# Weight conversion with its low bits taken by ScalarE, head 0 multiplied in plain float32, and a new set of due times

## The chip, the core and the metric

The kernel runs on one core of one Trainium2 chip. The metric is the device time of one execution in microseconds (us). The engines are named as the profile names them: PE is TensorE's matmul, PEld its weight load, DVE is VectorE, ACT is ScalarE, POOL is GpSimd, SP is SyncE, which issues the transfers (DMA).

## What is computed

Two batches of eight heads, 768 tokens of 64 numbers, go through an attention that is masked by clusters, and its output goes through two feed-forward stages. All weights (w1, w2, w3, w_out, w_in and w_out of the second stage) arrive as float64 and are turned into float32 on the chip.

```python
q_assign = argmax(einsum('bhsd,hcd->bhsc', q_n, c_n))      # 16 centroids per head
k_assign = argmax(einsum('bhsd,hcd->bhsc', k_n, c_n))
mask = q_assign[:, :, :, None] == k_assign[:, :, None, :]
scores = where(mask, scale * q @ k^T, -1e9)
attn = softmax(scores)
x = (attn @ v)                 # 1536 tokens x 512
h = (x @ w1) * (x @ w2) @ w3   # d_ff 1024
x = h @ w_out
h = x @ w_in                   # second stage, d_ff 2048
out = (h * clip(h + 3, 0, 6) / 6) @ w_out
```

## The kernel before

Nearly every float32 operand of a matmul is split into a high part (fp32r, written by ACT, sometimes POOL) and a low part (operand minus high part, written by DVE or POOL). A product of two split operands is three matmuls (high-high, high-low, low-high), a product with one split operand is two.

**The attention, per head** (`prep_ops`, `attn_ops`; 16 heads). q and k are transposed on PE (L1171), split (L1178, L1181), the cluster codes are worked out on DVE and POOL (L1224 to L1240). For each of six blocks of 128 queries, `scores` (L1309) fills 768 columns of PSUM, `smax` takes the maximum on DVE (L1321), `sexp` the exponentials on ACT (L1328). The probabilities are transposed on PE in nine groups of four 128x128 blocks (`p_T`, L1344). `p_hi` (L1346) copies each group to the fp32r tile `ph` on ACT, `p_lo` (L1351) writes the rest to `pl` on DVE; both move 128x512. `v_hi` and `v_lo` (L1158, L1164) put the high part of v in one half of the 128 columns of the tile `vs` and the low part in the other. `av` (L1354) multiplies: six calls for each head, in each two blocks, each with `ph` and with `pl`, so 24 matmuls of 384 columns for a head.

**The weights** (`conv_ops`, L1525). 72 tiles of 128x512 float64 numbers: 8 of w_out ("wo"), 16 of w3, 16 of w1 and w2 ("ab"), 32 of the second stage ("set"). A tile is loaded into `raw` (two 32-bit words a number), and then goes through five instructions: `c_bias` (c0, ACT) scales the high word, read as a float, into `cvt`; `c_clamp` (c1, POOL or DVE) clamps it in place; `c_shift` (c3, DVE, L1544) shifts it left by 3 into `cvs`; `c_low` (c4, DVE, L1548) ors in the low word shifted right by 29; `c_sign` (c5, DVE, L1552) ors in the sign. `raw`, `cvt` and `cvs` have two buffers each. c4 gives the `raw` buffer back (six tiles of w_out lie in a larger `rawx`), c5 gives back `cvt`. In the program, c3, c4 and c5 carry `lock=True`: the planner doesn't let them start while it thinks POOL is at work.

**The stages.** The weights w3 and w_out of the first feed-forward stage are multiplied with each other (`w_mm`, L1599) and the products of x with w1 and w2 (`ab_mm`, L1675) are made for batch 0 while the attention still runs (to about 384 us). Then come the two x2 products (`x2_mm`, L1790), batch 1's first stage (`b_mm`, L1927), and from 511 us on the second stage (`h_mm`, L2238, and `o_mm`, L2282). `idle_pe` (L1096) are matmuls without use, placed at the start.

**The order.** Each step is declared with `op` (key, engine, planned duration, what it needs, a due time, the buffers that it takes and gives back). `Plan.order` (L868) lays all steps out one by one: of the steps that can start at about the earliest time on each engine it takes the one with the earliest due time. A due time is a formula plus an entry of the table `SHIFT` (L44), some 3,700 numbers. The resulting order is fixed in the program: each engine runs its instructions strictly in that order. Steps declared with `fop` may go to more than one engine, as `RUN_ON` allows, and the planner chooses; c1 has "dp" (DVE or POOL).

Of the kernel before, what the change touches and what calls it, by code (L numbers as in the profile page):

```python
# [8 lines left out]
F32 = mybir.dt.float32  # L9
F32R = mybir.dt.float32r  # L10
I32 = mybir.dt.int32
AF = mybir.ActivationFunctionType
# [32 lines left out]
    "id": -11.08, "root": 17.17, "z": -42.97, "cenl": -6.79, "cen1": 13.45, "cen2": -5.32, "cen3": -2.8,  # L45
    ("idle", 0): 18.01, ("idle", 1): -7.42, ("idle", 2): -8.49, ("idle", 3): -0.46, ("idle", 7): 0.9,
    ("idle", 8): -9.34, ("cT", 0): -4.5, ("cTc", 0): -13.8, ("cTc", 1): -0.45, ("lq", 0): -10.38, ("lk", 0): -53.5,
    ("lv", 0): -30.2, ("vhi", 0): -8.63, ("vlo", 0): 28.32, ("T", 0, 0): -49.19, ("qkh", 0, 0): -18.28,
    ("qkl", 0, 0): -25.79, ("T", 0, 1): -28.46, ("qkh", 0, 1): -31.56, ("qkl", 0, 1): 15.3, ("Dk", 0): -25.47,
# [2340 lines left out]
```

## Time and profile before

| | |
|---|---|
| device time, median of 3 runs | 769.05 us (767.98 to 769.82) |
| the profiled execution | 768.52 us, of which the span from the first to the last instruction is 766.7 us |
| busy in the span | PE 737.8, PEld 673.3, DVE 648.0, ACT 511.1, POOL 212.0 us |
| mean granted TensorE clock | 0.994 of full speed |
| HBM read, written | 71.34 MB, 15.78 MB |

A group of instructions is shown with its line in the program, its engine, what it writes and reads, how many there are, the sum of their time and the mean of one; then the idle time of the engine just before them and who ended it. Many copies share the lines L990 (DVE subtraction) and L993 (ACT copy), since helpers issue them; they are told apart by their tiles. The ends of matmuls are modelled, and two that overlap in PE's pipeline each show their full length, so the time that a matmul takes of PE is read from how many follow each other in a stretch.

### The profile page before, as it was taken

Reading aid. Unit: us, or ns where it says so; the run is one execution under the profiler, and the core shown is the slowest. Engines: PE = TensorE matmul, PEld = TensorE weight load, DVE = VectorE, ACT = ScalarE, POOL = GpSimd, SP = SyncE. Lnnn points to the kernel's source line nnn. Section 1 sums busy time; section 2 is a strip of 40 time slices with the busy share of each in tenths; the row PEclk is TensorE's granted clock in tenths of the full one; section 3 lists DMA queues with packets and bytes.
Section 4 is the critical chain, followed back from the end, with each engine's and each line's share of the span. In section 5 each row is a group of like instructions: output and inputs, shape, how many; then the busy total and the mean of one; then the engine's idle time right before and its main releaser. Section 6 shows DMA issues by size and latency. Waiting matters only on the chain.

```text
span 766.7 us, 12083 instructions
## 1 busy us (share of the span) xinstructions
PE 737.8 (96%) x4143; PEld 673.3 (88%) x4143; DVE 648.0 (85%) x1114; ACT 511.1 (67%) x963; POOL 212.0 (28%) x233
## 2 busy tenths in 40 slices
...
PEclk9899999999999999999999999999999999999999
...
GB/s 241 187 139 128 130 156 150 107 128 143 115 203 130 194 161 146 139 110 68 136 121 152 179 97 165 105 225 140 164 163 153 111 121 168 97 42 42 71 12 83
DMA packets 81741, 101.97 MB, mean 133 GB/s; under 512 B 30960, under 2 KB 56592, under 8 KB 81680
## 3 DMA queue, kind: packets, MB, share of 16 engines
...
q14 instruction: 28, 0.23, 0.1%
HBM read 71.34 MB, written 15.78 MB: 114 GB/s over the span
## 4 chain that ended last, share of the span: by engine, by line
PE 80%; DVE 11%; ACT 3%; issue 2%; DMA 2%; POOL 0%; SPq 0%; DVEq 0%; ACTq 0%
PE po L2282 15%; PE psh L2238 13%; PE psx L1790 8%; PE psab L1675 8%; PE psab L1927 7%; PE pst L1309 7%; PE av L1361 7%; PE ptr L1344 6%; PE psw L1599 4%; DVE pl L990 2%; DVE den L1321 2%; DMA abp<-cvs 1%; PE pa L1210 1%; PE ptqk L1171 1%; DVE cvs L1548 1%
## 5 line engine op out<-in xcount | busy, mean ns | idle before, releaser
L1539 POOL TENSOR_SCALAR cvt<-cvt 128x512 f32<-128x512 f32 x72 | 70.4, 980 | 238.1 <-ACT cvt L993 207.9
L1328 ACT ACTIVATE p<-pst,den 128x768 f32<-128x768 f32 x96 | 86.6, 902 | 29.6 <-DVE den L1321 29.0
L1321 DVE TENSOR_REDUCE den<-pst 128x1 f32<-128x768 f32 x96 | 91.1, 949 | 13.4 <-PE pst L1309 10.1
L990 DVE TENSOR_TENSOR pl<-ptr,ph 128x512 fp32r<-128x512 f32 x144 | 96.2, 680 | 6.8 <-ACT ph L993 6.3
L993 ACT ACTIVATE ph<-ptr 128x512 fp32r<-128x512 f32 x144 | 83.4, 596 | 26.5 <-PE ptr L1344 23.5
L1344 PE MATMUL ptr<-id_f,p 128*128 128x128 f32 x576 | 82.1, 272 | 2.7 <-DVE pl L990 2.7
L1675 PE MATMUL psab<-xT,abhl 128*128 128x384 f32 x384 | 80.1, 343 | 2.5 <-DVE g L1685 2.5
L1344 PEld LDWEIGHTS ptr<-id_f,p 128*128 128x128 f32 x576 | 68.5, 140 | 9.6 <-issue 3.5
L1309 PE MATMUL pst<-kk,qkL 128*128 128x512 f32 (+1 forms) x192 | 71.0, 376 | 3.7 <-ACT p L1328 2.8
L1675 PEld LDWEIGHTS psab<-xT,abhl 128*128 128x128 f32 x384 | 65.7, 188 | 5.2 <-DVE g L1685 3.7
L1361 PE MATMUL av<-ph,vs 128*128 128x384 f32 x192 | 67.8, 353 | 0.5 <-issue 0.4
L1361 PE MATMUL av<-pl,vs 128*128 128x384 f32 x192 | 65.2, 340 | 2.1 <-DVE pl L990 2.1
L1309 PE MATMUL pst<-kk,qkH 128*128 128x512 f32 (+1 forms) x192 | 64.8, 341 | 1.9 <-ACT kk L993 1.9
L993 ACT ACTIVATE cvt<-raw 128x512 f32<-128x512 f32 x72 | 48.3, 673 | 13.1 <-DMA raw<-in_moe_w_dram 6.5
L1548 DVE SCALAR_TENSOR_TENSOR cvs<-raw,cvs 128x512 int32<-128x512 int32 x72 | 51.1, 713 | 0.5
L1552 DVE SCALAR_TENSOR_TENSOR cvs<-cvt,cvs 128x512 int32<-128x512 int32 x72 | 50.6, 705 | 0.3
L1599 PE MATMUL psw<-woh,wT 128*128 128x512 f32 x128 | 50.0, 409 | 0.2 <-DVE wT L990 0.2
L993 ACT ACTIVATE m_sn<-psh 128x384 f32<-128x384 f32 x64 | 31.0, 484 | 28.5 <-PE psh L2238 28.3
L2260 ACT ACTIVATE tt<-m_sn,three 128x384 f32<-128x384 f32 x48 | 29.4, 616 | 28.7 <-DVE m_sn L2248 19.7
L1544 DVE TENSOR_SCALAR cvs<-cvt 128x512 int32<-128x512 int32 x72 | 37.7, 527 | 11.1 <-POOL cvt L1539 4.2
L1309 PEld LDWEIGHTS pst<-kk,qkL 128*128 128x128 f32 x192 | 36.4, 189 | 10.9 <-ACT p L1328 8.9
L2282 PE MATMUL po<-m_hl,m_gv 128*128 128x512 f32 x171 | 43.8, 391 | 0.0
...
## 6 DMA issues: line engine op xcount, KB each, us to landing
...
```

Of the source, the lines that this page charges most:

```text
L990: nc.vector.tensor_tensor(out=out, in0=a, in1=b, op=ALU.subtract)
L993: nc.scalar.activation(out=out, in_=in_, func=AF.Copy, **kw)
L1309: x = mm(out=psr[:, t, ks_], lhsT=TT[nm, h][:, i, cs_], rhs=flat(TT["K", h][:, a])[:, ks_], start=st, stop=sp)
L1321: done["mx", n] = [other_banks(nc.vector.tensor_reduce(out=den_at(h, 0, c), in_=psS[h, c], axis=AX.X, op=ALU.max, negate=True), ("S", n + 1))]
L1328: done["ex", n] = [other_banks(nc.scalar.activation(out=flat(p), in_=psS.pop((h, c)), func=AF.Exp, bias=den_at(h, 0, c), accum_out=den_at( ...
L1344: nc.tensor.transpose(pt[:, blk(j)], pps[h, 3 * hf + c][:, blk(kb)], id_f)
L1361: mm(out=t[:, 0:HF], lhsT=vs_t[h][:, 2 * s + i, :], rhs=x_[:, c0:c0 + HF], start=(s == 0 and i == 0 and n == 0), stop=(s == 2 and i == 1 a ...
L1539: (nc.gpsimd.tensor_scalar if e == "pool" else ts)(out=tf, in0=tf, scalar1=H_MAX, scalar2=-H_MAX, op0=ALU.min, op1=ALU.max)
L1599: mm(out=ps, lhsT=wT[m, hf][:, a, blk(kk)], rhs=w_[hf][:, kk, :], start=(kk == 0 and n == 0), stop=(kk == 3 and n == 2))
L1675: mm(out=ps[:, 0:HF], lhsT=s[:, w, a, blk(kk)], rhs=xT0[0][:, x_, kk, hf * HF:hf * HF + HF], start=(kk == 0 and n == 0), stop=(kk == KD - ...
L2238: mm(out=ps[:, 0:HF], lhsT=left(p, l, a, kk), rhs=x[:, x_, kk, :], start=(st and kk == 0 and m == 0), stop=(kk == 1 and m == 2), skip_grou ...
L2282: mm(out=outs[b, c], lhsT=g[:, a, blk(c % 3)], rhs=w[:, w_, :], start=(first and a == 0 and w_ == 0), stop=(last and a == 1))
```

## The change

1. `c_low` moves from DVE to ACT and becomes step c2: it reads the top byte of the low word as an 8-bit integer (`raw` as bytes, every eighth byte), computes byte/32 - 15.5/32 and writes the result, rounded to an integer, into `cvs`. It needs c0, takes the `cvs` buffer and gives back `raw`. `c_shift` (c3) now both shifts the high word and ors the result with what c2 wrote, one instruction with two inputs, and so needs c1 and c2. c5 follows c3. DVE has two instructions for a tile where it had three, ACT two where it had one.
2. Head 0 (`WHOLE = 1`): `p_all` copies each transposed group to a float32 tile `p32` on ACT (in place of `p_hi`), there is no `p_lo`, v is copied whole to a float32 `vs` and the other half of the columns is set to zero by a POOL memset (in place of `v_lo`), and `av` is one float32 matmul for each block in place of two fp32r ones: 12 for 24. The group's PSUM buffer is given back by the ACT copy.
3. The second q/k transpose of a head is ordered after the first (`after=[("T", h, 0)] * hf`).
4. Every number of the table `SHIFT` is another one, so the fixed order of all engines is laid out anew.

```diff
     def v_hi(e, h):
-        t = at.tile([128, NC, 128], F32R, tag="vs", name="vs", bufs=2)
+        t = at.tile([128, NC, 128], F32 if h < WHOLE else F32R, tag="vs", name="vs", bufs=2)
...
     def v_lo(e, h):
         hi, lo = 64 * (h % 2), 64 - 64 * (h % 2)
+        if h < WHOLE:
+            nc.gpsimd.memset(vs_t[h][:, :, lo:lo + 64], 0.0)
+            return
         sub_on(e, vs_t[h][:, :, lo:lo + 64], v_n[h], vs_t[h][:, :, hi:hi + 64])
...
+    def p_all(h, n):
+        if not P32:
+            P32.append(at.tile([128, 1536], F32, tag="p32", name="p32"))
+        copy_act(P32[0][:, p_cols(n)], phl.pop((h, n)))
...
-            for n, x_ in enumerate(PHL):
+            ps_ = P32 if h < WHOLE else PHL
+            for n, x_ in enumerate(ps_):
                 mm(out=t[:, 0:HF], lhsT=vs_t[h][:, 2 * s + i, :], rhs=x_[:, c0:c0 + HF],
...
+        def c_low(e):
+            s = cvo[key] = base.tile([128, 512], I32, tag="cvs", name="cvs", bufs=2)
+            copy_act(s, raws.pop(key).bitcast(U8)[:, :, 3], scale=1.0 / 32.0, bias=-15.5 / 32.0)
+
         def c_shift():
-            s = cvo[key] = base.tile([128, 512], I32, tag="cvs", name="cvs", bufs=2)
-            ts(out=s, in0=cvt[key], scalar1=3, scalar2=None, op0=ALU.logical_shift_left)
-
-        def c_low():
             s = cvo[key]
-            stt(out=s, in0=raws.pop(key)[:, :, 0], scalar=29, in1=s, op0=ALU.logical_shift_right, op1=ALU.bitwise_or)
+            stt(out=s, in0=cvt[key], scalar=3, in1=s, op0=ALU.logical_shift_left, op1=ALU.bitwise_or)
...
-        op(("c3",) + key, "dve", 0.335, c_shift, (("c1",) + key,), due=due - 1.2, take=("cvs",), lock=True)
-        op(("c4",) + key, "dve", 0.602, c_low, (("c3",) + key,), due=due - 1.1, drop=(ring,), lock=True)
-        op(("c5",) + key, "dve", 0.602, c_sign, (("c4",) + key,), due=due - 1.0, drop=("cvt",), lock=True)
+        op(("c2",) + key, "act", 0.58, lambda: c_low(None), (("c0",) + key,), due=due - 1.25, take=("cvs",), drop=(ring,))
+        op(("c3",) + key, "dve", 0.602, c_shift, (("c1",) + key, ("c2",) + key), due=due - 1.2, lock=True)
+        op(("c5",) + key, "dve", 0.602, c_sign, (("c3",) + key,), due=due - 1.0, drop=("cvt",), lock=True)
```

## Rows read from the trace of the kernel before

**Rows 1.** The page: its first part, and the granted clock of its second.

```profile
PE 737.8 (96%) x4143; PEld 673.3 (88%) x4143; DVE 648.0 (85%) x1114; ACT 511.1 (67%) x963; POOL 212.0 (28%) x233
...
PEclk9899999999999999999999999999999999999999
```

**Rows 2.** Busy time by stretch: start:end, length, PE PEld DVE ACT POOL us (instructions), clock, DMA.

```profile
0.00:40.00 40.00, 26.63 (x106) 20.55 (x107) 31.27 (x66) 21.46 (x38) 19.74 (x47) 0.91 0.80 206
40.00:100.00 60.00, 59.42 (x368) 52.90 (x367) 54.57 (x94) 47.57 (x96) 21.25 (x27) 1.00 0.49 136
100.00:160.00 60.00, 54.56 (x330) 46.19 (x328) 58.98 (x98) 46.83 (x94) 25.02 (x29) 1.00 0.52 145
160.00:220.00 60.00, 58.46 (x360) 50.89 (x359) 56.85 (x94) 45.25 (x92) 25.55 (x26) 1.00 0.53 134
220.00:280.00 60.00, 58.32 (x375) 55.60 (x374) 53.71 (x91) 45.88 (x94) 28.34 (x30) 1.00 0.61 173
280.00:340.00 60.00, 59.39 (x380) 56.03 (x380) 51.34 (x89) 44.33 (x89) 25.16 (x29) 1.00 0.46 131
340.00:400.00 60.00, 59.35 (x358) 56.95 (x357) 51.97 (x80) 42.80 (x77) 22.90 (x13) 1.00 0.35 113
400.00:460.00 60.00, 60.00 (x348) 60.00 (x347) 54.22 (x101) 33.02 (x61) 9.41 (x9) 1.00 0.42 136
```

**Rows 3.** The page's fourth part: the chain that ended last, by engine.

```profile
PE 80%; DVE 11%; ACT 3%; issue 2%; DMA 2%; POOL 0%; SPq 0%; DVEq 0%; ACTq 0%
```

**Rows 4.** Waits: engine and line waiting <- releaser: us in total, times, longest.

```profile
ACT p L1328 <- DVE den L1321: 29.0, 30, 3.2
...
PEld pst L1309 <- ACT p L1328: 8.9, 19, 2.0
...
DVE cvs L1544 <- DMA abp<-cvs: 3.8, 2, 2.4
```

**Rows 5.** Groups by line: the five conversion instructions.

```profile
L1539 POOL TENSOR_SCALAR cvt<-cvt 128x512 f32<-128x512 f32 x72 | 70.4, 980 | 238.1 <-ACT cvt L993 207.9 <-DVE m_sn L2252 15.4 <-DVE m_gB L990 10.4
...
L1548 DVE SCALAR_TENSOR_TENSOR cvs<-raw,cvs 128x512 int32<-128x512 int32 x72 | 51.1, 713 | 0.5
L1552 DVE SCALAR_TENSOR_TENSOR cvs<-cvt,cvs 128x512 int32<-128x512 int32 x72 | 50.6, 705 | 0.3
...
L993 ACT ACTIVATE cvt<-raw 128x512 f32<-128x512 f32 x72 | 48.3, 673 | 13.1 <-DMA raw<-in_moe_w_dram 6.5 <-DVE cvs L1552 2.1 <-DMA raw<-in_moe_w_out_dram 1.3
...
L1544 DVE TENSOR_SCALAR cvs<-cvt 128x512 int32<-128x512 int32 x72 | 37.7, 527 | 11.1 <-POOL cvt L1539 4.2 <-DMA abp<-cvs 3.8 <-DMA set<-cvs 2.2
```

**Rows 6.** The tile cvt: its shift, nanoseconds min/median/max.

```profile
L1544 DVE TENSOR_SCALAR cvs<-cvt x72: 360/419/2080, 8.5 to 610.4; 128x512 int32<-128x512 int32 x72
```

**Rows 7.** Line L1544 by stretch, DVE: first four stretches.

```profile
0.00:40.00 40.00, 4.80 (x7) 0.91 0.80 206
40.00:100.00 60.00, 2.97 (x7) 1.00 0.49 136
100.00:160.00 60.00, 4.89 (x7) 1.00 0.52 145
160.00:220.00 60.00, 3.65 (x5) 1.00 0.53 134
```

**Rows 8.** Groups by line: head 0's subtraction and split of v, and a POOL memset.

```profile
L990 DVE TENSOR_TENSOR pl<-ptr,ph 128x512 fp32r<-128x512 f32 x144 | 96.2, 680 | 6.8 <-ACT ph L993 6.3
...
L987 POOL TENSOR_TENSOR vs<-vn,vs 128x384 fp32r<-128x384 f32 x16 | 16.9, 1054 | 1.1
...
L1066 POOL MEMSET cT<- 128x1056 f32 x1 | 1.0, 977 | 0.0
```

**Rows 9.** The chain in order of time: start, us, runs of matmuls back to back.

```profile
45.18 1.31 PE ptr L1344 x12
...
77.72 1.39 PE av L1361 x8
...
384.85 28.08 PE psx L1790 x162
```

More of the change, by code (lines that the diff above doesn't have):

```diff
@@ L11 @@
 I32 = mybir.dt.int32
+U8 = mybir.dt.uint8
 AF = mybir.ActivationFunctionType
@@ L44 @@
 SHIFT = {
[L45 to L49, printed above, removed]
[16 rows of a table removed]
@@ new lines @@
+    ("bsm", 7, 1): 3.11, ("bsm", 7, 2): 2.14, ("bsm", 7, 3): 27.32, ("blh", 7, 0): 17.71, ("bll", 7, 0): -23.76,
+    ("blh", 7, 1): 14.18, ("bll", 7, 1): -24.09, ("blh", 7, 2): 14.85, ("bll", 7, 2): -25.27, ("b", 7, 0, 0): -3.76,
[25 rows of a table added]
+    ("c2", "set", 0, 0): 1.24, ("c3", "set", 0, 0): 23.81, ("c5", "set", 0, 0): 30.14, ("sst", 0, 0): 19.07,
+    ("ld", "set", 0, 1): 50.16, ("c0", "set", 0, 1): 48.36, ("c1", "set", 0, 1): 24.86, ("c2", "set", 0, 1): 48.27,
+    ("c3", "set", 0, 1): 0.12, ("c5", "set", 0, 1): 16.9, ("sst", 0, 1): 39.01, ("ld", "set", 1, 0): 34.74,
@@ new lines @@
+    ("c0", "set", 1, 0): 10.87, ("c1", "set", 1, 0): 31.09, ("c2", "set", 1, 0): 52.71, ("c3", "set", 1, 0): 11.83,
+    ("c5", "set", 1, 0): 9.27, ("sst", 1, 0): 27.68, ("ld", "set", 1, 1): 16.36, ("c0", "set", 1, 1): 17.21,
+    ("c1", "set", 1, 1): 40.4, ("c2", "set", 1, 1): 24.8, ("c3", "set", 1, 1): 33.69, ("c5", "set", 1, 1): 26.12,
+    ("sst", 1, 1): 15.73, ("ld", "set", 2, 0): 15.92, ("c1", "set", 2, 0): 11.92, ("c2", "set", 2, 0): 14.04,
+    ("c3", "set", 2, 0): 16.28, ("c5", "set", 2, 0): -0.36, ("sst", 2, 0): 55.36, ("ld", "set", 2, 1): 31.61,
@@ new lines @@
+    ("c0", "set", 2, 1): 55.78, ("c1", "set", 2, 1): 13.05, ("c2", "set", 2, 1): 13.85, ("c3", "set", 2, 1): -14.33,
+    ("c5", "set", 2, 1): 29.88, ("sst", 2, 1): 0.23, ("ld", "set", 3, 0): 44.21, ("c0", "set", 3, 0): 28.62,
+    ("c1", "set", 3, 0): -4.58, ("c2", "set", 3, 0): 24.27, ("c3", "set", 3, 0): 32.62, ("c5", "set", 3, 0): 52.98,
+    ("sst", 3, 0): 33.94, ("ld", "set", 3, 1): 43.23, ("c0", "set", 3, 1): 10.53, ("c2", "set", 3, 1): 36.28,
+    ("c3", "set", 3, 1): 40.1, ("c5", "set", 3, 1): 2.37, ("sst", 3, 1): 34.35, ("ld", "set", 4, 0): 22.97,
@@ new lines @@
+    ("c0", "set", 4, 0): 19.3, ("c1", "set", 4, 0): 41.57, ("c2", "set", 4, 0): 40.62, ("c3", "set", 4, 0): 19.66,
+    ("c5", "set", 4, 0): 32.65, ("sst", 4, 0): 50.65, ("ld", "set", 4, 1): 41.54, ("c0", "set", 4, 1): 23.02,
+    ("c1", "set", 4, 1): -0.6, ("c2", "set", 4, 1): 11.39, ("c3", "set", 4, 1): 40.15, ("c5", "set", 4, 1): 31.09,
+    ("sst", 4, 1): 58.99, ("ld", "set", 5, 0): 21.02, ("c0", "set", 5, 0): 16.88, ("c1", "set", 5, 0): 17.4,
+    ("c2", "set", 5, 0): 20.09, ("c3", "set", 5, 0): 9.28, ("c5", "set", 5, 0): 15.04, ("sst", 5, 0): -3.23,
@@ new lines @@
+    ("ld", "set", 5, 1): 57.66, ("c0", "set", 5, 1): 39.57, ("c1", "set", 5, 1): 74.27, ("c2", "set", 5, 1): 66.57,
+    ("c3", "set", 5, 1): 68.7, ("c5", "set", 5, 1): 63.45, ("sst", 5, 1): -0.47, ("ld", "set", 6, 0): 47.69,
+    ("c0", "set", 6, 0): 61.48, ("c1", "set", 6, 0): 44.57, ("c2", "set", 6, 0): 19.7, ("c3", "set", 6, 0): 47.51,
+    ("c5", "set", 6, 0): 29.98, ("sst", 6, 0): 47.25, ("ld", "set", 6, 1): 42.89, ("c0", "set", 6, 1): 14.4,
+    ("c1", "set", 6, 1): 19.07, ("c2", "set", 6, 1): 2.94, ("c3", "set", 6, 1): 43.11, ("c5", "set", 6, 1): 43,
@@ new lines @@
+    ("sst", 6, 1): 15.31, ("ld", "set", 7, 0): 11.75, ("c0", "set", 7, 0): 17.06, ("c1", "set", 7, 0): 2.4,
+    ("c2", "set", 7, 0): 13.38, ("c3", "set", 7, 0): 9.33, ("c5", "set", 7, 0): -5.8, ("sst", 7, 0): -0.86,
+    ("ld", "set", 7, 1): 37.43, ("c0", "set", 7, 1): 9.21, ("c1", "set", 7, 1): 34.18, ("c2", "set", 7, 1): 40.94,
+    ("c3", "set", 7, 1): 33.33, ("c5", "set", 7, 1): 14.01, ("sst", 7, 1): 32.48, ("ld", "set", 8, 0): 54.98,
+    ("c0", "set", 8, 0): 7.4, ("c1", "set", 8, 0): 7.58, ("c2", "set", 8, 0): 10.67, ("c3", "set", 8, 0): 66.03,
@@ new lines @@
+    ("c5", "set", 8, 0): 22.54, ("sst", 8, 0): 73.76, ("ld", "set", 8, 1): 59.97, ("c0", "set", 8, 1): 42.12,
+    ("c1", "set", 8, 1): 50.56, ("c2", "set", 8, 1): 57.64, ("c3", "set", 8, 1): 28.65, ("c5", "set", 8, 1): 57.57,
+    ("sst", 8, 1): 49.24, ("ld", "set", 9, 0): 58.95, ("c0", "set", 9, 0): 4.02, ("c1", "set", 9, 0): 42.36,
+    ("c2", "set", 9, 0): 65, ("c3", "set", 9, 0): 33.1, ("c5", "set", 9, 0): 0.63, ("sst", 9, 0): 62.92,
+    ("ld", "set", 9, 1): 69.69, ("c0", "set", 9, 1): 15.23, ("c1", "set", 9, 1): 75.91, ("c2", "set", 9, 1): 59.5,
@@ new lines @@
+    ("c3", "set", 9, 1): 59.28, ("c5", "set", 9, 1): 57.41, ("sst", 9, 1): 27.13, ("ld", "set", 10, 0): 49.25,
+    ("c0", "set", 10, 0): 57.6, ("c1", "set", 10, 0): 19.16, ("c2", "set", 10, 0): 66.2, ("c3", "set", 10, 0): 2.52,
+    ("c5", "set", 10, 0): 2.52, ("sst", 10, 0): 45.24, ("ld", "set", 10, 1): 61.28, ("c0", "set", 10, 1): 15.56,
+    ("c1", "set", 10, 1): 61.42, ("c2", "set", 10, 1): 68.59, ("c3", "set", 10, 1): 25.49,
+    ("c5", "set", 10, 1): 49.93, ("sst", 10, 1): 35.86, ("ld", "set", 11, 0): 55.16, ("c0", "set", 11, 0): 39.3,
@@ new lines @@
+    ("c1", "set", 11, 0): 61.81, ("c2", "set", 11, 0): 39.85, ("c3", "set", 11, 0): 26.49,
+    ("c5", "set", 11, 0): 16.49, ("sst", 11, 0): 58.58, ("ld", "set", 11, 1): 61.28, ("c0", "set", 11, 1): -4.68,
+    ("c1", "set", 11, 1): 38.65, ("c2", "set", 11, 1): 60.23, ("c3", "set", 11, 1): 62.95,
+    ("c5", "set", 11, 1): 61.88, ("sst", 11, 1): 56.54, ("ld", "set", 12, 0): 49.18, ("c0", "set", 12, 0): 49.07,
+    ("c1", "set", 12, 0): 36.28, ("c2", "set", 12, 0): 49.22, ("c3", "set", 12, 0): 55.99,
@@ new lines @@
+    ("c5", "set", 12, 0): 27.37, ("sst", 12, 0): 2.05, ("ld", "set", 12, 1): 20.75, ("c0", "set", 12, 1): 19.56,
+    ("c1", "set", 12, 1): 47.09, ("c2", "set", 12, 1): 31.47, ("c3", "set", 12, 1): 15.05,
+    ("c5", "set", 12, 1): 25.67, ("sst", 12, 1): 25.49, ("ld", "set", 13, 0): 52.99, ("c0", "set", 13, 0): 33.65,
+    ("c1", "set", 13, 0): 48.84, ("c2", "set", 13, 0): 53.02, ("c3", "set", 13, 0): 22.47,
+    ("c5", "set", 13, 0): 35.55, ("sst", 13, 0): 19.2, ("ld", "set", 13, 1): 40.49, ("c0", "set", 13, 1): 53.77,
@@ new lines @@
+    ("c1", "set", 13, 1): 36.85, ("c2", "set", 13, 1): 15.25, ("c3", "set", 13, 1): 24.8,
+    ("c5", "set", 13, 1): 29.95, ("sst", 13, 1): 40.21, ("ld", "set", 14, 0): 55.15, ("c0", "set", 14, 0): 27,
+    ("c1", "set", 14, 0): 35.34, ("c2", "set", 14, 0): 72.48, ("c3", "set", 14, 0): 55.2,
+    ("c5", "set", 14, 0): 57.92, ("sst", 14, 0): 59.02, ("ld", "set", 14, 1): 42.15, ("c0", "set", 14, 1): 40.21,
+    ("c1", "set", 14, 1): 11.05, ("c2", "set", 14, 1): 32.32, ("c3", "set", 14, 1): 40.6,
@@ new lines @@
+    ("c5", "set", 14, 1): 10.64, ("sst", 14, 1): 56.62, ("ld", "set", 15, 0): 49.74, ("c0", "set", 15, 0): 52.29,
+    ("c1", "set", 15, 0): 60.32, ("c2", "set", 15, 0): 63.29, ("c3", "set", 15, 0): 54.04,
+    ("c5", "set", 15, 0): 46.69, ("sst", 15, 0): 61.27, ("ld", "set", 15, 1): 52.08, ("c0", "set", 15, 1): 7.04,
[52 rows of a table added]
+    ("xwh", 0, 1): 38.81, ("xwl", 0, 1): 0.22, ("xwh", 0, 2): 12.36, ("xwl", 0, 2): 2.09, ("xs", 0, 3): -0.19,
+    ("xwh", 0, 3): -2.71, ("xwl", 0, 3): -1.35, ("xs", 0, 4): 2.73, ("xwh", 0, 4): 19.74, ("xwl", 0, 4): -4.07,
```

187 lines of the change are left out of this document (67 added, 120 removed), and 1392 rows, old and new, of the table SHIFT.

## The prediction

> **What bounds the kernel now.** I read the page's first part, then the busy time by stretch, then the chain and the waits, and last the groups of the lines that change. PE is busy for 737.8 of 766.7 us [rows 1], so 28.9 us is all the idle time that the page shows on it, and any gain has to come out of that or out of stalls that the modelled ends of matmuls hide. By stretch [rows 2] the idle time is in few places: 13.4 us of the first 40, 0.6 in 40 to 100, 5.4 in 100 to 160, 1.5 in 160 to 220, 1.7, 0.6 and 0.7 in the three after it, nothing in 400 to 460. The place to look at is 100 to 160. There DVE is busy for 58.98 of 60 us and PE issues 330 matmuls; in 40 to 100, where the kernel does the same kinds of work, DVE is busy for 54.57 and PE issues 368; in 160 to 220, DVE 56.85 and 360. PE loses matmuls where DVE is full. The chain says the same of the whole: 80% of it lies on PE, 11% (84 us) on DVE, 3% on ACT [rows 3]. And ACT waits 29.0 us for DVE's maxima, while PE's loads wait 8.9 us for ACT's exponentials [rows 4]: the loop of scores, maximum and exponential is late on DVE first. After 400 us PE is full whatever the others do.
>
> **The conversion.** For each of 72 tiles DVE had the shift (527 ns mean), the or of the low word (713) and the sign (705); it now has a two-input shift-and-or and the sign [rows 5]. The new instruction has the form of the two that stand there, two int32 inputs of 128x512, so I take 0.71 us, and what goes is the shift: 72 x 0.527 = 37.7 us of DVE. The bounds: on a quiet DVE the shift took 0.42 us (median, up to 2.08) [rows 6], so 72 x 0.42 = 30 us at least, and 37.7 where its long ones go too. By stretch it goes as 4.8 us in the first 40, 3.0 in 40 to 100, 4.9 in 100 to 160, 3.7 in 160 to 220 [rows 7], 26 of the 72 tiles; some 28 tiles lie after 400, where DVE's time buys almost nothing.
>
> ACT gets 72 instructions that read `raw` at the same stride as c0's: 0.673 us each [rows 5], with DVE's 0.713 for the old or as the upper bound, 48.5 us in all (51 at most). In 100 to 160 seven tiles make 46.8 + 4.7 = 51.5 of 60 us, 86%; in 40 to 100, 47.6 + 4.7 = 52.3, 87% [rows 2, 7]. That is under the 91% of DVE in 40 to 100, where PE hardly stalled. After the change both engines stand at 86 to 90% there, in place of 98 and 78.
>
> The trace has ACT slower than DVE for what was removed (0.673 against 0.42 to 0.53) and with room, and DVE faster and without room. The Trainium skill ("ScalarE: Activation LUTs", Rules for kernel authors) says that additions and multiplications belong on VectorE, not on ScalarE. By that rule the 48.5 us on ACT against 37.7 on DVE would be a loss of 11 us; the rows speak for the move in 100 to 160, since there the engine counts that is full. That the rule may win is the second rival below.
>
> What the move does to waits. c3 now waits for c2 as well as for POOL's clamp. The clamp takes 0.98 us and c2 0.67, both from the end of c0 [rows 5], so issued right behind c0 the new wait is covered by the clamp; if the order puts an exponential between, c3 is late, and behind it on DVE stand the maxima and the `pl` subtractions for which PE waits. c2 takes the `cvs` buffer that c3 took: DVE's waits for stores out of `cvs` (3.8 us for "ab" and 2.2 for "set" [rows 4, 5]) are now ACT's, ahead of its exponentials. In exchange `raw` is free two DVE instructions earlier, and the next load may start earlier; the loads share transfers that are busy for 0.35 to 0.61 of the time [rows 2], so I count nothing. All 72 clamps ran on POOL [rows 5]; if some go to the relieved DVE they take back about 0.4 us each (the fast form of [rows 6]).
>
> **Head 0.** Nine subtractions of 0.68 us leave DVE: 6.1 us [rows 8], between about 35 and 60 us, where DVE is at 91% and PE not idle. ACT's nine copies stay as they are. POOL's 1.05 us for v's low part becomes a memset of 384 columns, at the pace of the 1056 in 0.98 us about 0.36 [rows 8]; this is needed only by the first `av`, and I count it at nothing, at most 0.7 us either way. PE does 12 float32 matmuls for 24 fp32r ones. The old ones follow each other at 1.39/8 = 0.174 us (also 28.08/162 in the x2 stage) [rows 9], 4.2 us in all. No float32 matmul that isn't a transpose is in the trace. Lower bound: the new ones go at the old pace, 12 x 0.174 = 2.1, a gain of 2.1. The nearest row is the float32 transposes, 1.31/12 = 0.109 us for 128 columns [rows 9], so 0.33 for 384 and 3.9 us in all: a gain of 0.2. Upper bound: twice that pace, as at the half clock that the first 40 us show in part (mean 0.91 [rows 2]): 7.9 us, a loss of 3.7. I take the nearest row: 0. The stretch that would hide a loss, 40 to 100, has only 0.6 us of idle PE [rows 2], so what it costs is paid.
>
> The Trainium skill ("FP8 and Floating Point Precision", TensorE Precision Notes) gives true FP32 four passes through the array. By it the 12 take 12 x 0.695 = 8.3 us, 4.2 more than before, and the sum below would be 4 us later; the transposes' row shows 0.109 for 128 columns, 1.9 times the fp32r pace, so the trace shows no such factor for them.
>
> **The new order.** All numbers of `SHIFT` differ, so each engine's order is another. No row prices this; what can be won is bounded by PE's idle time and what can be lost is in the rivals. The ordering of the second transpose behind the first costs nothing: both are on PE and were laid out close to each other.
>
> **The sum**, stretch by stretch. First 40 us: 4.8 us of DVE's 31.3 go, but the head-0 chain there is made of latencies in turn (load, transposes, codes, scores); bounds 0 and 5, I take -2. 40 to 100: -0.5 (idle 0.6). 100 to 160: DVE falls from 59.0 to 54.1, the load of 40 to 100; if PE then issues as there, (368 - 330)/368 x 60 = 6.2 us are won, if only as in 160 to 220, 4.9; bounds -1 and -6.2, I take -5. 160 to 220: -1 (bounds 0 and -1.5). 220 to 400: half of 1.7 + 0.6 + 0.7, -1.5 (bounds 0 and -3). After 400: -0.5 (0 to -1). Head 0's matmuls: 0 (-2.1 to +3.7). ACT's extra load in the attention, some 44 tiles and the three waits that it inherits: +2 (0 to +10; the upper end is a third of 44 x 0.67 = 29.5). Together -8.5. From the profiled execution's 768.5 us, which is 0.5 below the median of 769.05 and holds 1.8 us outside the span, that gives **760.0 us**.
>
> **The rivals.** *First, DVE's time buys nothing*: PE is at 96%, the planner spends the freed time on clamps, and the stall of 100 to 160 stays because it is a chain of maximum and exponential. Against it stands the drop of 38 matmuls exactly where DVE is full; for it, that 40 to 400 shows only 10.5 us of idle PE in all. Gains of 3 and head 0's 0 to 3.7: 766 to 770. *Second, slower: ACT becomes late.* ACT runs in order, and PE's loads already wait 8.9 us for its exponentials [rows 4]. If a third of 44 x 0.67 shows on PE (+9.8) and head 0's upper bound is paid (+3.7), with 5 of the gains left: 768.5 + 9.8 + 3.7 - 5 = 777. It decides from where ACT passes DVE's present 95 to 98% in a stretch; by my count it reaches 87%, so it needs the new order to bunch the tiles. *Third, the start slips*: the new order leaves PE quieter in the first 40 us, the granted clock stays at 1.2 GHz longer than it does now, and the gain there becomes a loss of 3 to 5, with the rest of the gains halved: 768 to 773.
>
> **Chances.** Forecast 0.70 (its own range 751 to 766), first rival 0.12, second 0.13, third 0.05. The range that should hold the time 8 times in 10 reaches from 750 (all upper gains but the last few us: 5 + 0.6 + 6.2 + 1.5 + 3 + 1 + 2.1 = 19.4) to 769.5, so that it leaves out the slow rivals. Of the first rival 0.04 counts as faster by over 0.2% (about what a measurement of this kernel can tell from no change), 0.06 as the same, 0.02 as slower. Faster 0.74, the same 0.06, slower 0.20.
>
> **What would show it.** DVE about 40 us less busy (38 and 6, less clamps that it takes over), ACT about 48 more; in 100 to 160 DVE below 56 us, ACT above 50, and some 360 matmuls; no or fewer waits of c3 for stores, and such waits on ACT instead; head 0's `av` at 0.33 us a matmul. Wrong would be: ACT above 57 us in a stretch of the attention with PE's loads waiting for `p` for much more than 8.9 us; float32 matmuls at 0.7 us; a first 40 us with fewer than 106 matmuls or a lower clock than 0.91; PE issuing no more than now in 100 to 160 though DVE has room.

## The result, and the profile after

The changed kernel takes 762.1 us (median, 760.64 to 763.72) against 769.0: a ratio of 0.9911 [0.9887, 0.9935], 7 us faster, where 760.0 was forecast. The profiled execution of after is its slowest one, 763.72 us with a span of 761.8. It stands against before's 766.7, so the two traces differ by only 4.9 us.

The page of after: busy time of each engine, and the chain by engine.

```profile
PE 739.7 (97%) x4143; PEld 673.7 (88%) x4143; DVE 617.8 (81%) x1032; ACT 551.5 (72%) x1037; POOL 209.9 (28%) x232
...
PE 82%; DVE 6%; ACT 5%; DMA 4%; issue 2%; SPq 0%; POOL 0%; DVEq 0%; ACTq 0%; POOLq 0%
```

DVE lost 30 us, ACT gained 40, and DVE's part of the chain fell from the 11% of [rows 3] to 6%. The busy time by stretch of after, columns as in [rows 2]:

```profile
0.00:40.00 40.00, 29.38 (x132) 21.75 (x133) 30.13 (x61) 27.69 (x51) 16.01 (x43) 0.96 0.80 223
40.00:100.00 60.00, 59.96 (x350) 51.29 (x349) 51.19 (x83) 52.42 (x104) 26.90 (x33) 1.00 0.50 137
100.00:160.00 60.00, 56.93 (x341) 49.99 (x340) 55.80 (x93) 50.51 (x102) 21.59 (x27) 0.97 0.56 147
160.00:220.00 60.00, 59.97 (x378) 54.24 (x377) 55.11 (x92) 50.93 (x101) 27.79 (x29) 1.00 0.58 150
220.00:280.00 60.00, 60.00 (x388) 57.39 (x387) 51.88 (x87) 50.84 (x104) 23.01 (x27) 1.00 0.58 156
280.00:340.00 60.00, 59.38 (x371) 55.76 (x370) 48.25 (x80) 46.85 (x94) 29.54 (x31) 1.00 0.48 139
340.00:400.00 60.00, 59.41 (x358) 57.04 (x357) 51.56 (x78) 43.62 (x77) 18.64 (x10) 1.00 0.36 113
```

Added up against [rows 2], PE is 26 matmuls ahead at 40 us, 8 at 100, 19 at 160, 37 at 220, 50 at 280 and 41 at 400 (a count and not a time, since the matmuls differ in length). Where the gain goes after that is seen from when the stages begin: the tiles `psx` (the x2 product) and `psh` (the second stage) of before, and then of after. Columns: duration of one in ns (min/median/max), first to last start in us.

```profile
L1790 PE MATMUL psx<-gh,Whl x192: 334/334/334, 384.7 to 430.3; 128*128 128x384 f32 x192
...
L2238 PE MATMUL psh<-m_x,m_gB x168: 331/334/446, 510.8 to 624.2; 128*128 128x384 f32 x168
```

```profile
L1820 PE MATMUL psx<-gh,Whl x192: 334/334/446, 375.6 to 411.2; 128*128 128x384 f32 x192
...
L2268 PE MATMUL psh<-m_x,m_gB x168: 331/334/446, 502.4 to 615.8; 128*128 128x384 f32 x168
```

The attention ends 9.1 us earlier (by the first `psx`). The x2 and batch 1's stage give 0.7 back (126.1 to 126.8). The second stage, from the first `psh` to the last `po` matmul, gives back 3.9 (251.5 to 255.4). The tail behind it is 0.4 shorter: -9.1 + 0.7 + 3.9 - 0.4 = -4.9.

The granted clock at the start is part of what these traces show. In before it falls to half between 24 and 32 us, in after it falls for a shorter time between 16 and 24 us (0.79 there). Over the first 40 us it is 0.91 in before and e3 and 0.96 in e1, but 1.00 in e2 and e9, and all of them keep before's order; it is 0.96 in after and e11, but 1.00 in the other kernels with after's order. So the order alone doesn't set it, and a first `psx` below can carry a microsecond or two of it.

The waits of before and, after the dots, of after: DVE waiting for PE's scores, ACT for the maxima, then what PE's loads and the conversion wait for.

```profile
DVE den L1321 <- PE pst L1309: 10.1, 21, 1.4
...
DVE den L1344 <- PE pst L1332: 18.1, 28, 1.8
ACT p L1351 <- DVE den L1344: 16.9, 22, 2.4
...
PEld pst L1332 <- ACT p L1351: 8.0, 15, 1.4
...
DVE cvs L1578 <- ACT cvs L1013: 6.4, 5, 2.6
...
ACT cvs L1013 <- DMA set<-cvs: 5.2, 5, 2.0
```

ACT's wait for the maxima fell from 29.0 to 16.9 us, and DVE now waits 18.1 for PE's scores, for 10.1 before: in the loop of scores, maximum and exponential, DVE is no longer the late one. The wait for stores went from DVE to ACT as the prediction said.

### The profile page after: what moved, and what is told of

It is laid out like the page before. It is cut to its first block, busy times and chain, and to the rows that moved or that the text cites. A ratio compares the mean times of both kernels' runs of the same rounds, so it can differ in the third digit from the quotient of the medians.

```text
span 761.8 us, 12047 instructions
## 1 busy us (share of the span) xinstructions
PE 739.7 (97%) x4143; PEld 673.7 (88%) x4143; DVE 617.8 (81%) x1032; ACT 551.5 (72%) x1037; POOL 209.9 (28%) x232
## 4 chain that ended last, share of the span: by engine, by line
PE 82%; DVE 6%; ACT 5%; DMA 4%; issue 2%; SPq 0%; POOL 0%; DVEq 0%; ACTq 0%; POOLq 0%
PE po L2312 15%; PE psh L2268 13%; PE av L1390 8%; PE psx L1820 8%; PE pst L1332 8%; PE ptr L1367 7%; PE psab L1705 7%; PE psab L1957 7%; PE psw L1629 5%; DMA qkn<-in_k_dram 1%; PE pa L1233 1%; PE ptqk L1194 1%; DVE den L1344 1%; PE pt L1601 1%; DMA rdb<-rd 1%
## 5 line engine op out<-in xcount | busy, mean ns | idle before, releaser
L1569 POOL TENSOR_SCALAR cvt<-cvt 128x512 f32<-128x512 f32 x72 | 67.3, 938 | 192.0 <-ACT cvt L1013 178.1
L1344 DVE TENSOR_REDUCE den<-pst 128x1 f32<-128x768 f32 x96 | 91.5, 953 | 22.8 <-PE pst L1332 18.1
L1351 ACT ACTIVATE p<-pst,den 128x768 f32<-128x768 f32 x96 | 86.6, 902 | 17.8 <-DVE den L1344 16.9
L1010 DVE TENSOR_TENSOR pl<-ptr,ph 128x512 fp32r<-128x512 f32 x135 | 89.4, 680 | 9.4 <-ACT ph L1013 9.1
L1013 ACT ACTIVATE ph<-ptr 128x512 fp32r<-128x512 f32 x135 | 78.7, 596 | 18.6 <-PE ptr L1367 13.8
L1390 PE MATMUL av<-pl,vs 128*128 128x384 f32 x180 | 61.3, 341 | 2.3 <-DVE pl L1010 2.3
L1390 PE MATMUL av<-ph,vs 128*128 128x384 f32 x180 | 63.3, 351 | 0.2 <-ACT T L1013 0.2
L1578 DVE SCALAR_TENSOR_TENSOR cvs<-cvt,cvs 128x512 int32<-128x512 int32 x72 | 52.4, 735 | 12.7 <-ACT cvs L1013 6.4
L1013 ACT ACTIVATE cvs<-raw 128x512 int32<-128x512 uint8 x72 | 47.9, 673 | 6.7 <-DMA set<-cvs 5.2
L1582 DVE SCALAR_TENSOR_TENSOR cvs<-cvt,cvs 128x512 int32<-128x512 int32 x72 | 51.2, 719 | 0.4
L2312 PE MATMUL po<-m_whl,m_gv 128*128 128x512 f32 x153 | 40.6, 392 | 0.6 <-DVE m_gv L1010 0.6
```

The costliest lines, as they stand in the source:

```text
L1010: nc.vector.tensor_tensor(out=out, in0=a, in1=b, op=ALU.subtract)
L1013: nc.scalar.activation(out=out, in_=in_, func=AF.Copy, **kw)
L1344: done["mx", n] = [other_banks(nc.vector.tensor_reduce(out=den_at(h, 0, c), in_=psS[h, c], axis=AX.X, op=ALU.max, negate=True), ("S", n + 1))]
L1351: done["ex", n] = [other_banks(nc.scalar.activation(out=flat(p), in_=psS.pop((h, c)), func=AF.Exp, bias=den_at(h, 0, c), accum_out=den_at( ...
L1390: mm(out=t[:, 0:HF], lhsT=vs_t[h][:, 2 * s + i, :], rhs=x_[:, c0:c0 + HF], start=(s == 0 and i == 0 and n == 0), stop=(s == 2 and i == 1 a ...
L1569: (nc.gpsimd.tensor_scalar if e == "pool" else ts)(out=tf, in0=tf, scalar1=H_MAX, scalar2=-H_MAX, op0=ALU.min, op1=ALU.max)
```

## The experiments

Three theories were set against each other: (T1) the gain is DVE's relief from the conversion; (T2) it is head 0's shorter start; (T3) it is the new order itself. "Old order" means the sequence of the kernel before, kept instruction by instruction on each engine; "new order" that of after.

**The two parts in the old order, and the order without the parts.** e1 changes the conversion alone, with the ACT copy where the shift stood; e2 head 0 alone; e3 both. e6 is the order of after with neither part, e4 with head 0's part only, e5 with the conversion's only.

e1, on before (the clamp, in its old place, comes before both):

```diff
-            ts(out=s, in0=cvt[key], scalar1=3, scalar2=None, op0=ALU.logical_shift_left)
+            copy_act(s, raws.pop(key).bitcast(U8)[:, :, 3], scale=1.0 / 32.0, bias=-15.5 / 32.0)
...
-            stt(out=s, in0=raws.pop(key)[:, :, 0], scalar=29, in1=s, op0=ALU.logical_shift_right, op1=ALU.bitwise_or)
+            stt(out=s, in0=cvt[key], scalar=3, in1=s, op0=ALU.logical_shift_left, op1=ALU.bitwise_or)
```

> The order of the kernel before is kept instruction by instruction; only the conversion is changed: where the shift stood in the order, ACT now writes the low bits, and where the or stood, DVE does the shift-and-or. Head 0 is split as before. Theory 1 (the gain is DVE's relief by the conversion): 762 to 766 us, DVE some 38 us less busy. Theory 2 (the gain is head 0's shorter start): 768 to 771. Theory 3 (the gain is the new order): 768 to 772.

e2 is the `vs`, memset, `p_all` and `av` part of the diff on before, with `p_lo` of head 0 left out of the sequence.

> The order of the kernel before is kept; only head 0 is changed: plain float32, no low part of its probabilities, a memset in place of the low part of its values. Theory 1: 769 to 774, since PE does 4.6 us more (the float32 matmuls of the changed kernel take 8.8 us for 4.2). Theory 2: 763 to 766. Theory 3: 768 to 772.

e3 is e1 and e2 together.

> The order of the kernel before with both changes. Theories 1 and 2: 761 to 766, most of the gain without any new due time. Theory 3: 768 to 773, nothing without them.

e4, on after:

```diff
-            copy_act(s, raws.pop(key).bitcast(U8)[:, :, 3], scale=1.0 / 32.0, bias=-15.5 / 32.0)
+            ts(out=s, in0=raws.pop(key)[:, :, 0], scalar1=29, scalar2=None, op0=ALU.logical_shift_right)
```

> The order of the changed kernel; only the low bits are taken by DVE again (a shift of the low word, where ACT read the byte). Theory 1: 768 or more, and PE loses matmuls in the attention. Theory 2 and theory 3: 761 to 765.

e5, on after: `vs` is fp32r again, the memset is v's low part again, and each `p_lo` of head 0 is put behind the next DVE step of the fixed order.

> The order of the changed kernel; only head 0 is split again, its nine subtractions one DVE instruction behind the copies. Theory 1 and theory 3: 758 to 763, since PE gets 4.6 us back while DVE has room. Theory 2: 765 to 769.

e6 is e4 and e5 together.

> The order of the changed kernel with neither of the two changes: DVE shifts the low word where ACT took the byte, so it has three instructions for a tile again, and head 0 is split, its subtraction one DVE instruction behind the copy. Theory 3: 762 to 766, the order alone holds the gain. Theory 1: 772 or more, since that order counts on a lighter DVE. Theory 2: 767 to 771.

Measured. The ratios are to runs of before beside each kernel (769.4 to 770.0 there). The two columns on the right are us in each kernel's profiled execution, read like the rows above.

| order, parts | median us | ratio to before | first `psx` | second stage |
|---|---|---|---|---|
| old, none (before) | 769.0 | 1 | 384.7 | 251.5 |
| old, conversion (e1) | 777.9 | 1.0104 [1.0073, 1.0135] | 391.0 | 253.0 |
| old, head 0 (e2) | 773.1 | 1.0041 [1.0023, 1.0059] | 388.6 | 252.2 |
| old, both (e3) | 779.1 | 1.0119 [1.0089, 1.0150] | 395.0 | 253.0 |
| new, none (e6) | 777.7 | 1.0100 [1.0068, 1.0132] | 384.9 | 258.5 |
| new, conversion (e5) | 765.1 | 0.9945 [0.9929, 0.9961] | 377.8 | 255.8 |
| new, head 0 (e4) | 776.0 | 1.0079 [1.0061, 1.0098] | 382.0 | 257.5 |
| new, both (after) | 762.1 | 0.9911 [0.9887, 0.9935] | 375.6 | 255.4 |

No theory stands alone: e2, e4 and e6 fell in T1's ranges and e5 in T2's, but e1 and e3 came out slower than every range that was expected of them. In the old order both parts lose (to `psx`: +6.3 and +3.9, together +10.3), and the new order without them loses as well, all of it behind the attention: its `psx` starts where before's does. In the new order the same parts gain 7.1 and 2.9, together 9.3. In device time the conversion is worth 13.9 us there (776.0 to 762.1; 12.9 by the ratios) and head 0 3.0 (765.1 to 762.1; 2.6 by the ratios, whose intervals just overlap). (e4's profiled execution was 2.2 us below its median and after's 1.6 above, so the traces of the pair show only 9.8 of the 13.9.) One limit of e4 and e6: they put DVE work into an order that was laid out without it, as e1 to e3 do with ACT.

**Why the old order loses.** The waits of e1 (its lines are 1 further than before's):

```profile
ACT p L1329 <- DVE den L1322: 23.6, 32, 1.7
DVE cvs L1549 <- ACT cvs L994: 14.9, 14, 3.6
PEld pst L1310 <- ACT p L1329: 13.4, 30, 2.0
```

DVE stands 14.9 us in front of the shift-and-or, with its maxima queued behind, because the copy comes late on ACT; and PE's loads wait 13.4 us for the exponentials in place of 8.9 [rows 4]. e9 takes the first away: the copy stands right behind c0, with four `cvs` buffers so that it needn't wait for one (place and buffers change together).

```diff
         def c_bias(e):
...
+            s = cvo[key] = base.tile([128, 512], I32, tag="cvs", name="cvs", bufs=NCVS)
+            copy_act(s, raws.pop(key).bitcast(U8)[:, :, 3], scale=1.0 / 32.0, bias=-15.5 / 32.0)
```

> The order of the kernel before, the conversion on ACT as in the run that lost 8 us, but ACT writes the low bits right behind its scaling of the high word, and cvs has four buffers so that it can (the small identity tile moves to another pool to make room). There DVE's shift-and-or waited 14.9 us for ACT's copy. If that place of the copy made the loss: 763 to 770, and the wait is under 3 us. If ACT's 48 us more are too much for that order wherever they stand: 774 to 779.

It took 771.9 us, 1.0017 [1.0001, 1.0032], between the two ranges. The waits of e9:

```profile
ACT p L1330 <- DVE den L1323: 17.9, 24, 1.7
PEld pst L1311 <- ACT p L1330: 15.3, 25, 3.0
...
PE pst L1311 <- ACT p L1330: 7.5, 14, 2.7
```

DVE's wait for the copy is gone, and of the 8.2 us that e1 lost against before 1.9 are left: DVE's maxima are in time (29.0 to 17.9), but the exponentials behind the copies on ACT are not, and PE waits for them for 15.3 and 7.5 us. DVE's relief was passed on to ACT: in this trace, of e9's fastest execution (769.6 us), the first `psx` starts at 384.8, where before's does.

**How dear ACT's time is.** e8 makes the copy twice in after, 48 us more of copies on ACT (34 us more of its busy time, 551.5 to 585.6).

```diff
-            copy_act(s, raws.pop(key).bitcast(U8)[:, :, 3], scale=1.0 / 32.0, bias=-15.5 / 32.0)
+            for _ in range(2):
+                copy_act(s, r, scale=1.0 / 32.0, bias=-15.5 / 32.0)
```

> The changed kernel, with each of the 72 copies of the low bits made twice on ACT: 48 us more of ACT, nothing more on DVE. If ACT still has room (the forecast's count): under 768. If ACT is now as full as DVE was (the second rival): 775 or more.

It took 785.7 us, 1.0223 [1.0196, 1.0250]: 23.6 us slower than after. By stretch, e8 in 100 to 160, and its waits:

```profile
100.00:160.00 60.00, 55.01 (x335) 46.75 (x334) 54.70 (x89) 54.56 (x110) 24.02 (x28) 1.00 0.51 139
```

```profile
PEld pst L1332 <- ACT p L1351: 20.6, 32, 2.0
...
DVE cvs L1580 <- ACT cvs L1013: 16.3, 15, 3.3
```

ACT shows 91% there, but this is read from a loop that has slowed down. At after's pace the nine copies that start in 40 to 100 us would add 9 x 0.57 = 5.1 to its 52.42 us: 57.5 of 60, 96%. (0.57 is what a copy takes of a busy ACT, from the starts in after's timeline of ACT; the durations of neighbours overlap:)

```profile
500.90 0.67 ACT L1013 ACTIVATE cvt<-raw 128x512 f32<-128x512 f32 x1 [1.99 <-DMA raw<-in_moe_w_in_dram]
501.48 0.66 ACT L1013 ACTIVATE cvs<-raw 128x512 int32<-128x512 uint8 x1
502.04 1.26 ACT L1013 ACTIVATE m_gB<-m_gb 128x1280 fp32r<-128x1280 f32 x1
```

By this count the stretch passes the 95% of the second rival; no row shows that share, since the loop slows first. What the trace does show is what that rival said would follow: PE's loads wait 20.6 us for exponentials in place of 8.0.

**Head 0's float32.** e7 is after with head 0's p and v in fp32r, multiplied once: the low parts of head 0's p and v are left out of the computation.

```diff
-        t = at.tile([128, NC, 128], F32 if h < WHOLE else F32R, tag="vs", name="vs", bufs=2)
+        t = at.tile([128, NC, 128], F32R, tag="vs", name="vs", bufs=2)
...
-            P32.append(at.tile([128, 1536], F32, tag="p32", name="p32"))
+            P32.append(at.tile([128, 1536], F32R, tag="p32", name="p32"))
```

> The changed kernel, with head 0's probabilities and values in fp32r and multiplied once: the low parts of head 0's product are left out. DVE and ACT do what they do in the changed kernel; PE's 12 products take one pass each. If PE pays for the float32 products (24 matmuls, 8.8 us in the changed kernel, against some 2.1): 755 to 758. If other waits cover them: 761 to 763.

The product in after's groups by line, and four of its matmuls back to back in the timeline of PE with what follows (start, us):

```profile
L1390 PE MATMUL av<-p,vs 128*128 128x384 f32 x24 | 8.8, 490 | 0.0
```

```profile
32.68 1.45 PE L1390 MATMUL av<-p,vs 128*128 128x384 f32 x4
33.97 0.60 PE L1367 MATMUL ptr<-id_f,p 128*128 128x128 f32 x4
```

Each of the 12 products shows as two matmuls, which is why PE's count is 4143 in both kernels. Four of them are followed after 33.97 - 32.68 = 1.29 us, 0.32 each, so a product takes 0.65 and the 12 take 7.7 us for the old 4.2 [rows 9]. e7 took 764.1 us, 0.9933 [0.9918, 0.9949], in neither range and no faster than after, and its `psx` starts at 375.4. Two stretches of e7, the second one the start of its second stage:

```profile
40.00:100.00 60.00, 57.38 (x345) 49.97 (x344) 52.95 (x85) 52.53 (x104) 26.49 (x32) 1.00 0.50 138
...
501.50:523.00 21.50, 19.59 (x93) 17.78 (x93) 19.11 (x30) 16.97 (x31) 6.63 (x6) 0.92 0.63 200
```

PE idles for 2.6 us where after shows 0.04: in the new order the float32 product is hidden, in front of exponentials for which PE would wait anyway. e10 below, which has the float32 product and the same start as e7 (first `av` at 30.5 and 30.6 us), begins head 1's `av` at 57.2 us, e7 at 57.1. In the old order the product isn't hidden: e2's `psx` is 3.9 us late, about the 3.5 that the product costs more. (e7's second stage is 257.6 us, which is where its 2 us lie. PE waits 1.6 us for ACT's `m_sn` at its start, for 1.0 in after, and then the granted clock falls: 0.92 over the 21.5 us of the row, some 1.7 us, where after shows 1.00.)

**The stretch 100 to 160.** After has 341 matmuls there, not 360. Its timeline (start, us; in brackets the idle time and who ended it):

```profile
119.30 1.83 POOL L1448 TENSOR_TENSOR T<-T,rdb 128x768 f32<-128x768 f32 x1
...
119.43 2.85 DVE L1582 SCALAR_TENSOR_TENSOR cvs<-cvt,cvs 128x512 int32<-128x512 int32 x2
...
122.20 0.94 DVE L1344 TENSOR_REDUCE den<-pst 128x1 f32<-128x768 f32 x1
...
123.07 1.27 DVE L1010 TENSOR_TENSOR pl<-ptr,ph 128x512 fp32r<-128x512 f32 x2
...
123.80 0.49 PE L1390 MATMUL av<-pl,vs 128*128 128x384 f32 x1 [2.26 <-DVE pl L1010]
```

The first of the two DVE instructions at 119.43 (in the tile `cvs`, 112 to 123 us, its line reads 679/1462/2245 ns) takes 2.245 us where such a one takes 0.72 on average. It begins 0.13 us behind a POOL multiplication of 128x768 and ends 0.5 us after it. The maximum and `pl` queue up behind it, PE stands for 2.26 us, and then, by small stretches of after:

```profile
118.00:124.00 6.00, 3.09 (x20) 2.43 (x19) 6.00 (x8) 4.24 (x8) 3.59 (x3) 1.00 0.16 51
124.00:126.00 2.00, 2.00 (x7) 1.71 (x7) 0.88 (x2) 2.00 (x5) 1.92 (x3) 0.51 0.00 0
126.00:128.00 2.00, 2.00 (x10) 1.72 (x9) 1.02 (x3) 1.03 (x3) 2.00 (x2) 0.63 0.00 0
```

Behind these six microseconds, of which PE was busy for 3.09, the granted clock falls to 1.2 GHz, for 3.4 us by the two rows. The Trainium skill ("SBUF — State Buffer", SBUF: two separate sides) says that GpSimd and a VectorE instruction with two SBUF inputs take one port pair in turn, each for its whole instruction. The trace agrees: 2.245 us is the 1.70 that are left of POOL's 1.83 plus 0.55, not quite one instruction. All seven kernels in the new order with POOL's long operations (after, e4 to e8, e11) have such an instruction of 2.21 to 2.27 us between 110 and 128 us; the granted clock falls behind it in all but e6 and e8. e10 cuts POOL's 128x768 additions, multiplications and subtractions (three helpers) into four pieces, in the order of after.

```diff
-        nc.gpsimd.tensor_tensor(out=out, in0=T, in1=rd, op=ALU.mult)
+        for i in range(0, 768, 192):
+            r = slice(i, i + 192)
+            nc.gpsimd.tensor_tensor(out=out[:, r], in0=T[:, r], in1=rd[:, r], op=ALU.mult)
```

> The changed kernel; POOL's additions, multiplications and subtractions of 128x768 in the attention are made in four pieces of 192 columns. In the changed kernel a DVE or with two SBUF inputs that began under such an operation took 2.24 us for 0.65, PE waited 2.26 us for the subtraction behind it, and the granted clock fell to half for 3.4 us. If DVE is held by the one long POOL instruction: no conversion instruction over 1.2 us there, no fall of the clock near 124 us, 759 to 761. If by POOL's traffic whatever its pieces: 762 to 764.

Its timeline at the same place, then the line of `cvs` for the pair (110 to 122 us) and the stretch 100 to 160:

```profile
117.34 1.69 DVE L1590 SCALAR_TENSOR_TENSOR cvs<-cvt,cvs 128x512 int32<-128x512 int32 x2
...
117.42 3.17 POOL L1453 TENSOR_TENSOR T<-T,rdb 128x192 f32<-128x192 f32 x4
...
120.55 0.45 PE L1390 MATMUL av<-pl,vs 128*128 128x384 f32 x1 [1.10 <-DVE pl L1010]
...
L1590 DVE SCALAR_TENSOR_TENSOR cvs<-cvt,cvs x2: 674/880/1086, 117.3 to 117.9; 128x512 int32<-128x512 int32 x2
...
100.00:160.00 60.00, 58.05 (x361) 50.87 (x360) 56.53 (x96) 53.15 (x107) 28.32 (x43) 1.00 0.57 154
```

The pair takes 1.69 us in place of 2.85, PE's stall is halved, the granted clock stays at 2.4 GHz and the stretch has 361 matmuls. The start isn't quite the same: here the pair begins 0.08 us ahead of POOL. It is the second of the two that begins under the pieces, and it takes 1.086 us; e12, with the same pieces, shows 1.085. Whole: 760.7 us, 0.9884 [0.9864, 0.9903], `psx` at 372.0. Of the 3.6 us to after's 375.6 some 2 lie ahead of this place (first `av` at 30.5 for 32.68, with the clock at 1.00 in the first 40 us for 0.96). Against e7, with e10's start but POOL's long operations, the first `psx` is 3.4 us earlier. The mechanism is shown where it was looked for; the intervals of e10 and after overlap, so a gain in device time isn't shown.

**The second stage.** e11 is after with before's due times for the steps of the second stage, as a test of whether the loss of 3.9 us lies in its order.

The edit is in the table alone: the entries of the second stage's steps (`h`, `o` and the steps that feed them) are before's, all others and the rest of the program are after's.

> The changed kernel with the due times of the kernel before for the steps of the second stage (h, o and what feeds them); the planner lays out anew. The changed kernel takes 259.4 us from the first matmul of that stage to the end, the kernel before 255.9. If the new due times of the stage cost this: 757 to 760. If it is ACT's additional copies for the last tiles: 761 to 766.

It took 765.3 us, 0.9938 [0.9923, 0.9954], in the range expected if ACT's copies were the cause; `psx` 375.5, second stage 257.2. But its timeline of PE shows what the time went into:

```profile
508.60 3.64 PE L1446 MATMUL psh<-m_x1b,m_gB 128*128 128x384 f32 x12 [4.36 <-ACT m_sn L191]
```

4.4 of the 257.2 us are this one stall, where the new order of the first part meets the old one of the second. Without it 252.8 would be left, the 251.5 to 253.0 of every kernel in the old order. (The granted clock falls behind the stall too, 0.92 over the first 21.4 us.) All other kernels in the new order need 255.2 to 258.5, those without ACT's copies too (e4, e6: 257.5 and 258.5), while the copies add 0.7 to 1.5 in the old order (252.2 to 253.0 in e1, e3 and e9). So most of the 3.9 us belong to the new order of the second stage and not to the copies on ACT; e4 and e6 carry DVE's extra shifts there, so the split isn't exact. That a seam without the stall would keep the 3 us wasn't tried. One piece of the new order's cost is the collision of 119 us again, in after's timeline:

```profile
575.87 2.01 POOL L1007 TENSOR_TENSOR m_whl<-x2f,m_whl 128x768 fp32r<-128x768 f32 x1 [22.80 <-ACT m_whl L1013]
...
576.10 2.20 DVE L1010 TENSOR_TENSOR m_gv<-tt,m_gv 128x384 fp32r<-128x384 f32 x1
...
578.35 0.50 PE L2312 MATMUL po<-m_whl,m_gv 128*128 128x512 f32 x1 [0.62 <-DVE m_gv L1010]
```

Two of the 41 `m_gv` subtractions start behind POOL's work here and take 2.20 us for a median of 0.55; in before the longest takes 0.56. e10's pieces leave these POOL operations whole, and its longest `m_gv` takes 2.21 us.

**A version that beats both.** e12 is e10 with three `cvs` buffers instead of two, since in after c2 waits for stores out of `cvs`.

```diff
-            s = cvo[key] = base.tile([128, 512], I32, tag="cvs", name="cvs", bufs=2)
+            s = cvo[key] = base.tile([128, 512], I32, tag="cvs", name="cvs", bufs=3)
```

> The changed kernel with POOL's pieces as in the run before last, and three cvs buffers for two in the same order: ACT's copies of low bits waited 6.4 us for stores out of cvs. If these waits on ACT, ahead of its exponentials, reach PE: 1 us or more under the run with the pieces alone. If not: within 1 us of it.

It took 759.18 us (758.75 to 760.11), 0.9862 [0.9843, 0.9882], below every time of after, and the two intervals don't overlap. ACT's waits for stores out of `cvs` (6.4 us in after) are gone from its waits. The median is 1.5 us under e10's, on the side where these waits reach PE, but e10's and e12's intervals overlap, so the third buffer's own share isn't shown. In 100 to 160 PE issues 360 matmuls, as in e10: that is the pieces' work.

## Why the prediction was nearly right

**The bound** was read rightly. DVE was the late engine of the attention, and taking the shift from it in an order that fits is worth the most of all parts (13.9 us).

**The sum up to 400 us** came out at -2 - 0.5 - 5 - 1 - 1.5 + 2 = -8; measured at the first `psx`, -9.1. Its terms fared worse than their sum, so that it came within 1.1 us is in part luck. The first 40 us gained more than the 2 forecast: the first `av` starts at 32.68, in before's timeline at 39.05, and PE has 26 matmuls more.

```profile
39.05 0.34 PE L1361 MATMUL av<-ph,vs 128*128 128x384 f32 x1
```

Some of this is the clock, which stays low for longer in before's trace than in after's. In 40 to 100, 18 of these are lost again (350 against 368); 15 of head 0's 24 float32 matmuls lie there. In 100 to 160 the load moved as forecast (DVE 55.8, ACT 50.5 against "below 56, above 50"), but PE won 11 matmuls, not 30, and its idle time went from 5.4 to 3.1 us. The step that failed is "if PE then issues as there": a stall of 2.26 us behind POOL's multiplication and 3.4 us at the lower clock behind it took the rest, and e10 gave it back. 160 to 280 gained 18 and 13 matmuls, more than forecast.

**Head 0** was costed at nothing from the transposes' 0.109 us [rows 9]. That choice failed: the product costs 0.65 us, at the upper bound. The sign "0.33 us a matmul" came out (0.32), but two matmuls make one product. The rate that the prediction quoted from the Trainium skill ("FP8 and Floating Point Precision", TensorE Precision Notes: four passes) was the better guide: 0.65 against 0.174 is 3.7 times. A float32 transpose is no measure for a float32 product. The sum was not hurt, for a second error: "what it costs is paid" holds in the old order (e2), not in the new one, where PE had slack in front of the exponentials (e7).

**ACT's load** was +2 within 0 to +10. The trace of after can't split that term. The second rival was close by: its waits came when the copy was doubled (e8), and also in e1, with ACT at 85% by the same count (before's 46.83 us in 100 to 160 [rows 2] and 7 copies of 0.57), where the order had the copies in the wrong places (8.2 us, of which e9's earlier copy took back 6.3). A share of busy time was thus not the whole of its condition. The rule of the Trainium skill weighed there ("ScalarE: Activation LUTs", Rules for kernel authors: additions and multiplications belong on VectorE) loses in the new order and wins in the old one.

**After 400 us** -0.5 was forecast and +4.2 came (0.7 + 3.9 - 0.4). This is the term that failed most. "No row prices this" was said of the new order, and its price was bounded by PE's idle time alone, as a gain. That a full PE can get stalls of its own was not counted. In the second stage PE waits 0.3 us in before (the first line) and 3.2 in after:

```profile
PE po L2282 <- DVE m_whl L990: 0.3, 1, 0.3
...
PE psh L2268 <- DVE m_sn L2278: 1.3, 3, 0.7
PE psh L2268 <- ACT m_sn L1013: 1.3, 2, 1.0
PE po L2312 <- DVE m_gv L1010: 0.6, 1, 0.6
```

**The small terms.** c3 and the new copy in after's groups by line:

```profile
L1578 DVE SCALAR_TENSOR_TENSOR cvs<-cvt,cvs 128x512 int32<-128x512 int32 x72 | 52.4, 735 | 12.7 <-ACT cvs L1013 6.4 <-POOL cvt L1569 3.8 <-ACT asb L1013 1.5
...
L1013 ACT ACTIVATE cvs<-raw 128x512 int32<-128x512 uint8 x72 | 47.9, 673 | 6.7 <-DMA set<-cvs 5.2 <-DMA abp<-cvs 1.2 <-POOL wol L1007 0.2
```

They measured 0.735 for 0.71 and 0.673 for 0.673, the memset 0.41 for 0.36. DVE fell by 30 us and ACT rose by 40, not 40 and 48: busy time counts overlapping neighbours once (a copy is 0.57 of it, 41 us in all), which the sum of durations did not; on DVE other groups grew besides (the tile `m_gv` from 23.2 to 26.3 us, mostly by the two of 2.20 us above). The loads' share of 0.35 to 0.61 leaves out the 0.80 of the first 40 us; nothing was built on it. All clamps stayed on POOL (x72 at its line in both). The first and third rival didn't happen: DVE's time bought 13.9 us, and the first 40 us are at 0.96 of the full clock, not below 0.91; since the same order shows both (0.91 to 1.00 in the old one), that sign tells little about an order.
